# GEGLU on one core with split products: half of a set of operand sums made on VectorE, unit 4's S3 T3 divided, and pass two's second products next to each other

## The chip, the core and the metric

The kernel runs on one core of a Trainium2 chip. The core has a matrix engine (TensorE, PE in the profile; its weight loads are listed apart as PEld), a vector engine (VectorE, DVE), a scalar engine (ScalarE, ACT) and a general engine (GpSimd, POOL). SyncE (SP) issues the DMAs here. The engines each run their own instructions in the order in which they were written and wait for each other by semaphores. The metric is the time of one execution on the device in microseconds, as a median over runs.

## The reference

```python
def reference(x, w_gate, w_up, w_down):
    g = jnp.einsum("bsd,df->bsf", x, w_gate)
    u = jnp.einsum("bsd,df->bsf", x, w_up)
    h = _gelu(g) * u
    return jnp.einsum("bsf,fd->bsd", h, w_down)
```

x is 2048 x 1024, w_gate and w_up are 1024 x 3584, w_down is 3584 x 1024, all bfloat16; `_gelu` is the tanh form.

## The kernel before

**Split products.** The matrix products are made by a Strassen-Winograd scheme: a product of two 2 x 2 block matrices takes seven block products in place of eight, on sums of blocks. The sums of weights are called S1 to S4, the sums of x T1 to T4 (`sums_s`, `sums_t`); `tb` is a copy of a block of x. Raw blocks are 16-bit, sums are f32 (in the matmul format fp32r). Some of the seven products are themselves divided once more in the same manner, into seven halves of two matmuls each (`inner`, `half`) in place of one product of four matmuls for each of the four outputs (`product`, `whole`).

**Passes and units.** x is two passes p of 1024 rows. The columns of w_gate and w_up are 14 units u of 256 columns. Units 0 to 2 are worked off singly, for one pass at a time (`items`, `unit`, `whole_p4`). From `JOINT = 3` on, both passes of a unit are worked off jointly: units 3 to 13, with the products S4 Tb (steps X1 to X7) and A22 T4 (K1 to K7) divided. From unit `DIVIDED7 = 5` on, S3 T3 (H1 to H7) is divided too; before that it is H2, H3 and H4, made of whole products (16 matmuls for both passes and both weights). Behind the units follows the product with w_down (`down`).

**Order.** The order inside a joint unit is a text, `SEQUENCE` (`SEQUENCE_FIRST` for unit 3), of which each word issues some instructions. Upper-case words are matmuls: `P1pi` and `S`, `G` are products of raw 16-bit blocks (P1: four words of four matmuls; `S0 S1` are the second raw products of pass one, `G0 G1` those of pass two), `P6pi`, `P5pi`, X, H and K are f32. Lower-case words are single steps of DVE and ACT: `y5`, `kz1`, `kz6`, `v11` and so on copy a bank (ACT); `e00`, `e10`, `e01` copy what has been added up so far in the bank z into the bank of another output (ACT); `ga`, `gb`, `ha`, `hb` are gelus (ACT); `x..`, `c11a`, `e11`, `e10y` add (DVE); `m..` multiply and issue the store (DVE, SP). A word with `-` belongs to the unit before. `@` words are side work (`side_work`): sums of weights on POOL, loads, stores.

z and y are two of the eight banks of accumulation memory: X1, X6, X7 and H1, H6, H7 add up in z, X5 and H5 stand in y; in the K products the two are exchanged. H7 adds into z behind `e10`, which reads it.

**Sums of sums.** To divide a product, the sums T must be split into further sums: for tb and t4 three sums n1, n2, n4 (`split_b`) and one more, written over b12 (`split_b_rest`), for each of two k; all on POOL, 128 x 512 each. For t3 this is `split_b3`, in three parts (0 and 1: three sums each, 2: the two rests): part 0 at `@t4.1` of the unit before `DIVIDED7`, parts 1 and 2 at `@s3` of that unit. The weights' side is `half_sums`, two sums of 128 x 256 in each of two parts, at `@tb`, `@t3`, `@t4`. The sums n have places of their own (`place_n`, `more_room`) or slots of a common ring of 58 (`slot`).

The split of tb's rest and of t4 stands in the last single item, (0, 1): in `p4`, around `whole_p4`, that is ten POOL instructions ahead of unit 3:

```python
            def p4(c12):
                times(p, 2 * u, 1, gelu(c12[0]), c12[1])
                if n == len(items) - 1:
                    split_b_rest("tb")
                    more_room()
                    split_b("t4")
                whole_p4(u, p, banks[0], ss[u], ahead_of_p4, behind_p4)
                if n == len(items) - 1:
                    split_b_rest("t4")
```

Lines of the profile: L127 is the one line that issues every matmul, L106 every DVE tensor operation, L109 every one of POOL, L123 a copy out of a bank on ACT, L364 a copy into a bank, L373 and L221 gelus.

Of the kernel before, what the change touches and what calls it, by code (L numbers as in the profile page):

```python
# [10 lines left out]
def kernel(  # L11
# [19 lines left out]
    ADD, SUB, MUL = ALU.add, ALU.subtract, ALU.mult  # L31
# [14 lines left out]
    NWARM = 7  # L46
    JOINT = 3
    AHEAD = {(0, -2): 2, (0, -1): 2, (0, 1): 1, (1, -2): 1}
    DIVIDED7 = 5
    STAY = range(11, 14)  # L50
    KEEPS = [(u, n) for u in range(5, NU) for n in range({7: 2, 9: 2, 11: 2, 13: 3}.get(u, 1))]
    H, Q, R2 = NJ // 2, N // 2, range(2)
# [55 lines left out]
    def pool(out, a, b, op):  # L108
        nc.gpsimd.tensor_tensor(out=out, in0=a, in1=b, op=op)  # L109
# [190 lines left out]
    def blocks(name, k):  # L300
        return [T[p][name][h + k] for h in (0, 2) for p in range(2)]

    def split_b(name):
        n = ns[name] = [[], [], [], []]
        for k in range(2):
            b11, b12, b21, b22 = blocks(name, k)
            n1, n2, n4 = [place_n() for _ in range(3)]
            pool(n1, b12, b11, SUB)
            pool(n2, b22, n1, SUB)
            pool(n4, b21, n2, SUB)  # L310
            for got, t in zip(n, (n1, n2, b12, n4)):
                got.append(t)

    def split_b_rest(name):
        for k in range(2):
            b11, b12, b21, b22 = blocks(name, k)
            pool(b12, b22, b12, SUB)

    def split_b3(part):
        n = ns.setdefault("t3", [[], [], [], []])  # L320
# [13 lines left out]
    def half(ps, lhs, rhs, fresh=False):  # L334
# [2 lines left out]

    SEQUENCE = (
# [7 lines left out]
    ).split()  # L346

    SEQUENCE_FIRST = (
# [4 lines left out]
    ).split()  # L353

    def joint_ops(u, E, F):
# [85 lines left out]

        if u < DIVIDED7:
            for name in ("H1", "H5", "H6", "H7", "e00", "e10", "e01", "y5", "e11", "e10y"):
# [482 lines left out]
    sums, ns = {}, {}  # L926
    items = [(1, 0), (2, 0), (2, 1), (1, 1), (0, 1)]
# [41 lines left out]
    def load_next(u):  # L969
        if u < NU:  # L970
            ws[u] = load_w(u, u % 2 == 1)
# [13 lines left out]
    def side_work(u, what):  # L985
        def made(kind, n):
            if (u, n) in keeps:
                kind(keeps[u, n])

        more = u + 1 < NU  # L990
        name, part = what[:2], int(what[3:]) if what[2:3] == "." else None
        if what == "start":
            if u == JOINT:
                load_next(u + 1)
            made(fetch_wd, 1)
        elif what == "keep":
            made(keep_whole, 0)
        elif what == "store":
            if more:
                made(store_made, 0)  # L1000
            made(fetch_wd, 2)
        elif what == "s3":
            if u == DIVIDED7:
                split_b3(1)
                split_b3(2)
            if u > JOINT:
                new_s(u, "s3")
        elif name == "tb":
            if u > JOINT:
                half_sums(u, name, part)  # L1010
        elif name == "t3":
            if u >= DIVIDED7:
                half_sums(u, name, part)
            if more and part == 1:
                made(keep_whole, 1)
            if not more and part == 0:
                made(store_made, 0)
        elif what == "t4.0" and not more:
            half_sums(u, name, 0)
            half_sums(u, name, 1)  # L1020
        elif what == "t4.1" and not more:
            for n in range(1, 3):
                made(keep_whole, n)
        elif name == "t4":
            half_sums(u, name, part)
            if u == JOINT and part == 0:
                fetch_next(u)
            if u == DIVIDED7 - 1 and part == 1:
                split_b3(0)
        elif name in ("s1", "s2", "s4"):  # L1030
            if more:
                new_s(u + 1, what)
        elif what == "late":
            made(store_made, 1)
            if u > JOINT:
                fetch_next(u)
        elif what == "end":
            load_next(u + 2)
        if not more:
            last_loads(what)  # L1040
# [27 lines left out]
    with tc.manual_schedule(engines={ENG.Activation}):  # L1068
        for n, (u, p) in enumerate(items):
            first = n == 0  # L1070
            def after_p5():
                at_p5(n)

            def aside(part):
                if first and part < 0:
                    rest_of_0(part + 2)
                if first and part == 0:
                    t.make("t4")
                for v in loads.get((n, part), ()):
                    ws[v] = load_w(v, True)  # L1080
                turn_some(AHEAD.get((n, part), 0))
                if (n, part) == (1, -2):
                    two_sums("t2", XL[:, KH:], "t1")
                    two_sums("t3", XL[:, KH:], XL[:, :KH])

            def mid():
                if "sa" not in ss[u]:
                    ss[u]["sa"] = sums_s(loaded(u), pool)["how"]["sa"](None)

            def ahead_of_p4():  # L1090
                if n == 0:
                    raw_of(2, 0, even, cc)()
                elif n == 1:
                    p1 = [raw_first(e, 1, loaded(v)) for e, v in ((Eb, 2), (D, 1))]
                    raw_second(K, 1, loaded(2))
                    finish_raw(2, 1, K, p1[0])

                    T[1]["tb"] = spots["tb"]
                    for k in range(KH):
                        nc.scalar.copy(out=spots["tb"][k], in_=XT[1, 1][KH + k])  # L1100
                    new_room(0, 1, *["t4"] * KH, *["n"] * 3)
                    two_sums("t4", xT[1][:, KH:], "t2")
                    new_s(0, "s1", "s2", "s3", "s4")

                    def second_half():
                        raw_second(K, 1, loaded(1))
                        finish_raw(1, 1, K, p1[1])

                    nxt["c11"] = second_half
                elif n == 3:  # L1110
                    raw_of(0, 1, Ea, D)()

            def behind_p4():
                if "c11" in nxt:
                    nxt.pop("c11")()

            def p4(c12):
                times(p, 2 * u, 1, gelu(c12[0]), c12[1])
                if n == len(items) - 1:
                    split_b_rest("tb")  # L1120
                    more_room()
                    split_b("t4")
                whole_p4(u, p, banks[0], ss[u], ahead_of_p4, behind_p4)
                if n == len(items) - 1:
                    split_b_rest("t4")

            if first:
                banks = odd, cc, dd
                late = lambda: add(cc, nxt["p1"])
            else:  # L1130
                banks = (Eb, D, K) if n == 3 else (Ea, K, D)
                late = None
            unit(u, p, banks, ss[u], late, after_p5, aside, mid, p4)
            ss[u].pop("sa")
            if n == 1:
                Ea, Eb, K, D = Eb, D, K, Ea
            elif n == 3:
                Ea, Eb, K, D = Ea, K, D, Eb

        E, F = [Eb, K], [D, Ea]  # L1140
        last = None
        for u in range(JOINT, NU):
            now = joint_ops(u, E, F)
            steps = SEQUENCE_FIRST if u == JOINT else SEQUENCE
            for name in steps:
                if name[0] == "@":
                    side_work(u, name[1:])
                elif name[0] != "-":
                    now[name]()
                elif last:  # L1150
                    last[name]()
            last = now
            E, F = F, E
        for name in SEQUENCE:
            if name[0] == "-":
                last[name]()
# [51 lines left out]
```

## Time and profile before

| what | value |
|---|---|
| median of three runs | 526.39 us (526.26 to 526.95) |
| the profiled execution | 526.39 us, span 524.6 us |
| granted clock of TensorE | 1.00 throughout |
| unit 3, 4, 5, 6 (between the first weight loads of each, 83.49 to 179.88) | 24.26, 24.34, 23.90, 23.89 us |
| POOL busy in units 5 and 6 | 23.43 and 23.27 us |
| ten POOL sums ahead of unit 3 | from 85.40 to 98.39 us |

The span is the time from the first to the last instruction of the program; 1.8 us of the measured time lie around it. The profile gives for each engine the share of busy time, the chain of instructions that ended last (each followed back to what released it), the waits, and the instructions in order of time. In groups of instructions the tile names follow the program: `bank` is a bank, `w` and `xT` are raw weights and raw x, `s` sums of weights, `h`, `t`, `n` places of sums of x.

### The profile page before, as it was taken

How to read it: one execution, taken by the hardware profiler on the slowest of the kernel's cores; microseconds unless marked ns; L12 is line 12 of the kernel's file. 1: busy time of each engine (PE TensorE's matmuls, PEld its weight loads, DVE VectorE, ACT ScalarE, POOL GpSimd, SP SyncE). 2: the span in 40 equal slices, each digit the busy share in tenths (PEclk: the TensorE clock that was granted, in tenths of full speed). 3: DMA queues.
4: the chain of work that ended last, by engine and by line, in shares of the span. 5: the costliest groups of instructions: out<-in, count | busy, mean ns of one | idle time of the engine just before them, and what ended most of it. 6: DMA issues, size and time to landing. Idle time of an engine off the chain costs nothing.

```text
span 524.6 us, 7866 instructions
## 1 busy us (share of the span) xinstructions
PE 518.7 (99%) x2356; PEld 368.0 (70%) x2389; DVE 390.6 (74%) x598; ACT 293.6 (56%) x542; POOL 336.9 (64%) x339
## 2 busy tenths in 40 slices
PE   9999999999999999999999999999999999999997
PEld 5576877767667676767677676754788885488887
DVE  2984553687888989897988889897789226967934
ACT  3556655676778687878787787851135602142430
POOL 1079999998999999999999999840000000000594
PEclk9999999999999999999999999999999999999999
DMA  9961323032625457373727444999976999993732
GB/s 252 213 166 52 89 84 111 32 109 92 191 81 181 123 180 230 112 239 111 233 92 231 163 159 159 343 374 415 385 259 212 394 398 353 392 327 101 238 133 71
DMA packets 102730, 105.91 MB, mean 202 GB/s; under 512 B 19360, under 2 KB 80800, under 8 KB 102688
## 3 DMA queue, kind: packets, MB, share of 16 engines
q1 hardware_dynamic: 102688, 105.41, 61.4%
q8 instruction: 19, 0.31, 0.3%
q14 instruction: 23, 0.19, 0.1%
HBM read 72.61 MB, written 29.62 MB: 195 GB/s over the span
## 4 chain that ended last, share of the span: by engine, by line
PE 98%; DMA 1%; issue 0%; SPq 0%; DVE 0%
PE bank L127 98%; DMA xn<-in_x_dram 1%; SPq L797 0%; PE bank L804 0%; DVE st L106 0%
## 5 line engine op out<-in xcount | busy, mean ns | idle before, releaser
L127 PE MATMUL bank<-h,s 128*128 128x512 f32 x500 | 132.6, 395 | 0.0
L109 POOL TENSOR_TENSOR q<-q 128x256 fp32r<-128x256 f32 x28 | 26.6, 984 | 144.4 <-DMA q<-td 143.8
L127 PEld LDWEIGHTS bank<-h,s 128*128 128x128 f32 x500 | 93.9, 188 | 21.1
L127 PE MATMUL bank<-xT,w 128*128 128x512 bf16 (+1 forms) x446 | 106.8, 376 | 1.5
L127 PEld LDWEIGHTS <-w 128*128 128x128 bf16 x504 | 45.4, 98 | 59.1 <-issue 11.9
L109 POOL TENSOR_TENSOR s<-w 128x512 fp32r<-128x512 bf16 (+1 forms) x76 | 77.8, 1040 | 10.4 <-DMA w<-in_w_gate_dram 10.3
L127 PE MATMUL bank<-t,s 128*128 128x512 f32 x276 | 76.5, 400 | 0.0
L127 PE MATMUL bank<-q 128*128 128x512 f32 x264 | 65.6, 390 | 0.0
L127 PEld LDWEIGHTS bank<-t,s 128*128 128x128 f32 x276 | 51.9, 188 | 12.1
L127 PEld LDWEIGHTS bank<-q 128*128 128x128 f32 x264 | 49.6, 188 | 10.4
L123 ACT COPY p<-bank 128x512 f32<-128x512 f32 x72 | 40.6, 589 | 28.9 <-PE bank L127 28.6
L106 DVE TENSOR_TENSOR q<-h,h 128x512 fp32r<-128x512 bf16 x56 | 38.3, 684 | 16.8 <-DMA h<-hd 16.8
L123 ACT COPY u<-bank 128x512 f32<-128x512 f32 x62 | 35.8, 589 | 21.1 <-PE bank L127 21.0
L109 POOL TENSOR_TENSOR s<-s,s 128x256 fp32r<-128x256 f32 x60 | 44.8, 769 | 1.6
L106 DVE TENSOR_TENSOR xz<-bank,xz 128x512 f32<-128x512 f32 x44 | 30.2, 691 | 18.2 <-PE bank L127 14.6
L127 PEld LDWEIGHTS <-h 128*128 128x128 bf16 x224 | 21.7, 98 | 26.5 <-issue 0.5
L109 POOL TENSOR_TENSOR s<-w,s 128x512 fp32r<-128x512 bf16 (+1 forms) x37 | 39.4, 1081 | 0.0
L109 POOL TENSOR_TENSOR s<-s,w 128x512 fp32r<-128x512 f32 (+1 forms) x37 | 37.3, 1024 | 0.9
L118 ACT CAST tb<-raw 128x512 fp32r<-128x512 bf16 x28 | 16.9, 632 | 36.0 <-DMA raw<-in_w_down_dram 26.5
L109 POOL TENSOR_TENSOR m<-raw,m 128x512 fp32r<-128x512 bf16 x28 | 34.5, 1234 | 2.2
L106 DVE TENSOR_TENSOR bank<-bank,u 128x512 f32<-128x512 f32 x49 | 33.7, 688 | 0.0
L106 DVE TENSOR_TENSOR v<-bank,v 128x512 f32<-128x512 f32 x44 | 29.2, 684 | 2.1 <-PE bank L127 1.7
(122 smaller groups left out, 911.7 us busy)
## 6 DMA issues: line engine op xcount, KB each, us to landing
raw<-in_w_down_dram SPq DMA_DIRECT2D x68, 256.0 KB, 4.0
q<-td SPq DMA_DIRECT2D x66, 256.0 KB, 5.4
td<-m SPq DMA_DIRECT2D x42, 256.0 KB, 2.8
hd<-o SPq DMA_DIRECT2D x80, 128.0 KB, 1.7
h<-hd SPq DMA_DIRECT2D x17, 512.0 KB, 6.9
hd<-h SPq DMA_DIRECT2D x30, 128.0 KB, 1.7
h<-hd SPq DMA_DIRECT2D x5, 768.0 KB, 9.0
out_dram<-st SPq DMA_DIRECT2D x30, 128.0 KB, 4.6
```

What stands on the lines that cost most here:

```text
L106: nc.vector.tensor_tensor(out=out, in0=a, in1=b, op=op)
L109: nc.gpsimd.tensor_tensor(out=out, in0=a, in1=b, op=op)
L118: nc.scalar.copy(out=t, in_=src)
L123: nc.scalar.copy(out=t, in_=ps)
L127: nc.tensor.matmul(ps, lhsT=lhs, rhs=rhs, start=start, stop=stop, skip_group_check=True)
```

## The change

`DIVIDED7` goes from 5 to 4: unit 4 makes H1 to H7 too, with its side work (the four half sums at `@t3`) and with `split_b3` one unit earlier, so that part 0 falls into unit 3 and parts 1 and 2 into unit 4.

`split_b` and `split_b_rest` take an engine and a choice of k. The ten sums of tb and t4 leave `p4` and stand at `@start` of unit 3: tb's rest (two) and t4's three sums for k = 0 on DVE, t4's three for k = 1 and t4's rest (two) on POOL.

`SEQUENCE` has another order in the middle. Before, with the side work left out: `H5 P511 c11b gb y5 m11a H6 H2 v11 m12a K1 e10 x11 G0 kz1 m12b H7 f1 H3 v00+ K6 e01 e11 G1 hb`. After: `H5 H6 y5 c11b gb e10 P511 m11a H2 K1 v11 m12a x11 f1 H7 kz1 m12b H3 v00+ G0 G1 K6 e01 e11 hb`. So G0 and G1 follow each other directly, H6 comes ahead of P511, `e10` ahead of P511 as well, and H7 comes directly behind K1. `SEQUENCE_FIRST` is only broken into lines in another way.

```diff
-    DIVIDED7 = 5
+    DIVIDED7 = 4
...
-    def split_b(name):
-        n = ns[name] = [[], [], [], []]
-        for k in range(2):
+    def split_b(name, eng=pool, some=range(2)):
+        n = ns.setdefault(name, [[], [], [], []])
+        for k in some:
             b11, b12, b21, b22 = blocks(name, k)
             n1, n2, n4 = [place_n() for _ in range(3)]
-            pool(n1, b12, b11, SUB)
-            pool(n2, b22, n1, SUB)
-            pool(n4, b21, n2, SUB)
+            eng(n1, b12, b11, SUB)
+            eng(n2, b22, n1, SUB)
+            eng(n4, b21, n2, SUB)
...
-    def split_b_rest(name):
-        for k in range(2):
+    def split_b_rest(name, eng=pool, some=range(2)):
+        for k in some:
             b11, b12, b21, b22 = blocks(name, k)
-            pool(b12, b22, b12, SUB)
+            eng(b12, b22, b12, SUB)
...
-        "x6y X4 xz7 P611 x00 v10 x01 sg H1 X3 @room ga @t3.1 x7y S1 u211 x10 "
-        "e00 H5 @t4.0 P511 @free c11b gb y5 m11a H6 @t4.1 H2 v11 m12a K1 e10 x11 G0 @s1 kz1 m12b "
-        "H7 f1 H3 v00+ K6 e01 @late e11 G1 hb @s2 e10y kz6 H4 v10+ K5 sh K2 ha2 v01+ K7 ky5 m11b "
...
+        "x6y X4 xz7 P611 x00 v10 x01 sg H1 X3 @room ga @t3.1 x7y S1 u211 x10 e00 H5 @t4.0 H6 y5 @free "
+        "c11b gb e10 P511 m11a H2 @t4.1 K1 v11 m12a x11 f1 @s1 H7 kz1 m12b H3 v00+ G0 G1 K6 e01 @late "
+        "e11 hb @s2 e10y kz6 H4 v10+ K5 sh K2 ha2 v01+ K7 ky5 m11b K3 @s4 K4 kz7 @end "
...
             if u == JOINT:
                 load_next(u + 1)
+                split_b_rest("tb", dve)
+                split_b("t4", dve, range(1))
+                split_b("t4", pool, range(1, 2))
+                split_b_rest("t4")
...
                 if n == len(items) - 1:
-                    split_b_rest("tb")
                     more_room()
-                    split_b("t4")
                 whole_p4(u, p, banks[0], ss[u], ahead_of_p4, behind_p4)
-                if n == len(items) - 1:
-                    split_b_rest("t4")
```

On the engines this comes to two matmuls fewer, seven DVE instructions and four ACT copies more, one POOL instruction fewer (five less, four more), and the same transfers in the same order on SP.

10 rows, old and new, of tables (SEQUENCE, SEQUENCE_FIRST) are left out of this document.

## The prediction

> **What bounds the kernel now.** I read the page first: its share of busy time, the chain that ended last, then who waited for whom, and last the stretches of single units.
>
> ```profile
> span 524.6 us, 7866 instructions
> PE 518.7 (99%) x2356; PEld 368.0 (70%) x2389; DVE 390.6 (74%) x598; ACT 293.6 (56%) x542; POOL 336.9 (64%) x339
> PE 98%; DMA 1%; issue 0%; SPq 0%; DVE 0%
> ```
>
> The reader is to see that TensorE (PE) is busy 99% of the span and that the chain is PE for 98%. It runs matmul after matmul, and nothing else sets the end. The waits of the weight loads confirm it:
>
> ```profile
> PEld L127 <- issue: 12.4, 47, 0.3
> DVE p L106 <- PE bank L127: 9.6, 1, 9.6
> ```
>
> The only repeated pause of the weight loads is 0.26 us ahead of a group of 16-bit loads, 47 times, and it is put down to no other engine. VectorE (DVE), by contrast, once sits idle for 9.6 us; that is at the end of the last single item, just ahead of unit 3. So a gain must come from fewer or closer matmuls, and a loss from an engine that newly comes too late for PE.
>
> The stretches of units 4, 5 and 6 (cut at the first weight load of each; unit 4 begins at 107.75):
>
> ```profile
> 107.75:132.09 24.34, 24.24 (x107) 17.09 (x108) 21.12 (x32) 16.99 (x32) 22.41 (x24) 1.00 0.28 87
> 132.09:155.99 23.90, 23.80 (x105) 16.72 (x107) 20.21 (x32) 18.42 (x35) 23.43 (x25) 1.00 0.44 137
> 155.99:179.88 23.89, 23.78 (x105) 16.72 (x106) 21.12 (x34) 18.55 (x35) 23.27 (x25) 1.00 0.45 144
> ```
>
> Columns are time, then busy time and count of PE, PEld, DVE, ACT, POOL, and the granted clock, which is 1.00. Unit 4, the last undivided one, lasts 24.34 us; the divided ones 23.89. GpSimd (POOL) works 23.3 of 23.9 us, so it is the engine to watch.
>
> The weight loads of unit 5 and of unit 3 in order of time (start, length, what, count):
>
> ```profile
> 92.88 1.41 PEld L127 LDWEIGHTS <-w 128*128 128x128 bf16 x8 [0.26 <-issue]
> ...
> 99.18 1.41 PEld L127 LDWEIGHTS <-w 128*128 128x128 bf16 x8 [0.26 <-issue]
> ```
>
> ```profile
> 146.45 0.55 PEld L127 LDWEIGHTS <-w 128*128 128x128 bf16 x4 [0.26 <-issue]
> ...
> 150.08 0.55 PEld L127 LDWEIGHTS <-w 128*128 128x128 bf16 x4 [0.26 <-issue]
> 150.74 1.11 PEld L127 LDWEIGHTS bank<-h,s 128*128 128x128 f32 x5
> 151.89 0.19 PEld L127 LDWEIGHTS bank<-w,s 128*128 128x128 f32 x1
> 152.35 0.55 PEld L127 LDWEIGHTS <-w 128*128 128x128 bf16 x4 [0.27 <-issue]
> ...
> 155.99 0.98 PEld L127 LDWEIGHTS <-w 128*128 128x128 bf16 x6 [0.26 <-issue]
> ```
>
> At 146.45, 150.08 and 152.35 stand three groups of four 16-bit matmuls: S1, G0 and G1. Between G0 and G1 there are only six f32 matmuls. In unit 3, which has the other sequence, S0 S1 and G0 G1 stand together as two groups of eight.
>
> **What a switch of type costs.** In long undisturbed runs the loads start 0.2267 us apart in f32 and 0.216 in 16 bit. From 150.08 to 152.35 lie 4 + 6 matmuls: 4 x 0.216 + 6 x 0.2267 = 2.224, and the trace has 2.274, 0.050 more. From 152.35 to 155.99 lie 4 + 12: 3.584 against 3.633, 0.049 more. So a group of four costs about 0.05 us: part at its head, part in the nine or so f32 loads behind it, which start 0.228 to 0.238 apart. Unit 3's groups of eight: 92.88 to 99.18 (8 + 20) 6.262 against 6.300, and 99.18 to 107.75 (8 + 30) 8.529 against 8.567: 0.038 each. Per unit: 106 matmuls make 32 x 0.216 + 74 x 0.2267 = 23.69, and 23.89 is measured: 0.20 for four groups.
>
> **The change, part by part.**
>
> Unit 4 divided: four whole products of four matmuls (16) become seven halves of two (14). Two f32 matmuls are gone: 24.34 - 23.89 = 0.45 us saved, which agrees with 2 x 0.2267. This is on PE's path.
>
> G0 next to G1 (units 4 to 13, ten units): one group fewer in each. Bounds: nothing, if an eight costs as much as two fours; and 0.050 + 0.049 - 0.038 = 0.061 by unit 3's eights, the nearest row. I take 0.05, a whole group's cost, because the f32 work behind the eights of unit 3 is another than in later units: 10 x 0.05 = 0.50 us.
>
> Five sums from POOL to DVE at unit 3's start: two of Tb's rest and three of T4. On POOL such a sum takes 1.27 to 1.30 us, so POOL has 6.4 us less. On DVE a sum of this shape takes 0.68 with POOL idle (q<-h,h). None of the type with both operands f32 in SBUF stands there but o<-v,v, which takes 0.68 to 1.59 beside POOL. Five thus take 3.4 to 7.9 us and begin when DVE is done with the last h, at 84.4; the next DVE step, c11a, starts at 94.02. They end by 92.3. The cover is the 9.6 us of waiting for PE; without it they would hold back c11a and, behind it, the seed of f0 that G0 needs. The first user of Tb's rest is X7, behind S0 S1 (92.88), and of T4's sums the K products (from 101.6).
>
> A rule that speaks against this, from the Trainium skill, page "SBUF — State Buffer", section "Who interferes with whom": a VectorE instruction with two SBUF inputs and a GpSimd instruction that reads SBUF exclude each other, and the later one waits for the whole of the other. The spread of o<-v,v (0.68 to 1.59) agrees. Strictly alternating, five pairs would take 5 x (1.29 + 0.69) = 9.9 us and end at 94.3, 0.3 us past c11a's start; the seed of f0 comes at 97.62 after a stretch in which DVE idles 1.3 us, so the sum stays the same by the rule.
>
> S3 T3 in unit 4: DVE gets two more steps (0.69 each), ACT four copies (0.59), in the unit where both have most room (DVE 21.1 of 24.3, ACT 17.0): nothing. POOL gets four half sums (0.75 + 2.1 = about 3.0), and the splitting of T3 comes one unit earlier: three sums (4.0) at unit 3's end instead of unit 4's, five (6.9) at unit 4's start instead of unit 5's. POOL against before: -6.4 at unit 3's start, -2.4 at its end, +4.5 ahead of unit 4's S3, +7.5 behind its four half sums, +3.5 at its end, -3.4 in unit 5. Who needs it: S3, now done at 111.09 to 113.4, moves to 115.6 to 117.9, and the first half sum to 118.7. In unit 5, H1 begins 13.2 us and H5 15.0 us behind the unit's start; in unit 4 that is 121.0 and 122.8. Some 4.1 us are left, against 1.7 where unit 5 does this now (145.45 to 147.11). Hidden; if the 6.4 were not given back, PE would stand 2.3 us once.
>
> New order of H6, y5, e10, P511, H2, K1, H7: this costs PE nothing itself, but H7 adds into the bank that e10 reads, so PE waits for e10 there. At present e10 ends at 173.89 (its row 173.29, 0.60) and the next load that needs it starts at 174.64: 0.75 to spare. In the new order y5 starts 0.65 behind H5's last load (as kz1 does behind K1: load 149.63, copy 150.28), and the gelu gb stands between y5 and e10. Chain: 0.65 + 0.48 (copy to gelu, 175.52 to 176.00) + 0.53 (gelu to copy, 100.11 to 100.64) + 0.60 = 2.26 behind H5's last load. On PE eleven loads lie between that and H7: 11 x 0.2267 = 2.49. It leaves 0.23; the trace has a load starting 0.13 behind ACT's end (122.18 to 122.31) with no pause. Zero, with 0.1 us to spare. Queued behind H7 are all later matmuls. K6 now stands behind G1, so that seven loads (1.59) instead of eleven lie between its last load and K7, which adds into the bank that kz6 copies: 0.65 + 0.59 = 1.24, so 0.35 are left of 1.2 (kz6's end at 153.19, K7's load at 154.39): zero too. P511 comes two loads and G0 four f32 loads later; behind G0 waits the gelu hb, whose product on DVE (178.66) starts 2 us after hb ends (176.60): hidden.
>
> DMA: SP issues the same transfers in the same order, with seven more waits for slots. The weights for unit 5 are issued at 104.49 and used from 132.09, so a few us there are hidden.
>
> Sum: 0.45 + 0.50 = 0.95 us less. The profiled execution took 526.39 with a span of 524.6 (1.8 around it), and 526.39 is also the median of the runs. So 525.44, or -0.18%.
>
> **Rivals.**
> 1. Groups gain by unit 3's row or somewhat more: 0.45 + 10 x 0.061 = 1.06, 525.33. For it: the eights are the same instructions. Against: what follows them differs. Some spread of a median (runs lie 526.26 to 526.95) adds to this case.
> 2. Only the two matmuls count, since the cost goes with the number of 16-bit loads: 525.94. Against it: 20 loads would then cost 0.25, and four groups with 32 loads cost 0.20 in all.
> 3. H7 waits for e10 (the slower side). If ACT is held up by one more of its instructions between H5 and e10 (0.48), PE stands 0.48 - 0.23 + 0.06 = 0.3 us in each of ten units: 525.44 + 3.1 = 528.5. It decides from 0.1 us of stall a unit, which eats the gain; from 0.2 the kernel is slower by more than can be measured. For: the spare time falls from 0.75 to some 0.1 to 0.2, and K7's from 1.2 to 0.35. Against: ACT is idle ahead of y5 and its durations hardly vary.
> 4. POOL too late in unit 4, since it is locked out by DVE: at most the 2.3 us above, 527.7. Against: 4.1 us to spare.
>
> **How the numbers follow.** About 0.2% (1.05 us) is what a measurement of this kernel can tell from no change. Forecast (525.35 to 525.8) 0.48; rival 1, 0.35; rival 2, 0.06; rival 3, 0.08; rival 4, 0.03. Faster by over 0.2%: rival 1 and a little of the forecast's lower edge, 0.37. Slower: rivals 3 and 4 where they pass the bound, 0.09. The rest, 0.54, is within. The range runs from 525.15 (rival 1 with 0.2 of spread) to 526.0 (rival 2).
>
> **What would show it.** After: some 37 pauses of the weight loads put down to issue in place of 47; unit 4 at 23.84 like all later ones, which fall from 23.89 by 0.04 to 0.06; the DVE's wait of 9.6 us cut to 2 to 6; no wait of PE for ACT ahead of H7, nor for POOL at H1 and H5 of unit 4. I am wrong if units of 24 us and more appear with a pause ahead of H7, or if the later units keep 23.89.

## The result and the profile after

| | before | after |
|---|---|---|
| median, 20 runs each | 526.70 us (526.26 to 527.45) | 525.84 us (525.16 to 526.47) |
| ratio | | 0.998, 95% interval 0.9974 to 0.9987 |
| span of the profiled execution | 524.6 us | 524.1 us |
| first weight load of unit 3 to the first behind unit 13 | 263.64 us | 262.59 us |
| unit 4 | 24.346 us | 23.833 us |
| each of units 5 to 12 | 23.893 us | 23.833 us |

The changed kernel is faster by 0.2%; the interval is 0.7 to 1.4 us of 526.7, and the medians lie 0.86 us apart. 525.44 was forecast, 0.95 us less than the 526.39 that before had then. One execution of a kernel further below, e2_old_order, took 1128.56 us and stands in no ratio. The units' lengths, here and below, are taken between the first weight loads of two units, in the one execution of each kernel that was profiled. Apart from single units that are named, they repeat to 0.001 us from unit to unit (units 9 and 12 of e4 differ by 0.007), and tell far more than the spread of the runs does.

The page after, the same three lines as before:

```profile
span 524.1 us, 7920 instructions
PE 519.8 (99%) x2387; PEld 368.7 (70%) x2387; DVE 396.7 (76%) x605; ACT 292.4 (56%) x546; POOL 335.4 (64%) x338
PE 98%; DMA 1%; SPq 0%; DVE 0%; issue 0%
```

PE still makes up 98% of the chain: nothing else sets the end. The weight loads show the two matmuls that are gone (2389 and 2387). The count of matmuls itself rises, from 2356 to 2387: some of their records are missing in the first trace. The span shrank by only 0.5 us, because these two executions differ at the start: the chain of waits in order of time has the first load of x in it, once 4.03 and once 4.60 us long (start, length, what; before first, after second).

```profile
2.12 4.03 DMA xn<-in_x_dram
```

```profile
2.13 4.60 DMA xn<-in_x_dram
```

So every clock reading after unit 0 is 0.57 us later in the second trace, at a step that the change does not touch: the same start of unit 3 lies between 83.38 and 84.34 in the ten traces. Lengths of stretches can be compared, starts cannot. From unit 3 to the end of unit 13, PE needs 1.053 us less.

The waits of the weight loads after:

```profile
PEld L127 <- issue: 8.9, 34, 0.3
PEld L127 <- DMA td<-m: 0.8, 3, 0.3
PEld L127 <- DMA w<-in_w_up_dram: 0.3, 1, 0.3
PEld L127 <- DMA out_dram<-st: 0.3, 1, 0.3
PEld L127 <- DMA hd<-h: 0.3, 1, 0.3
```

The pause ahead of 16-bit loads stands here too under the names of transfers that happened to land then; all lines together are 40 pauses, against 50 before (47 put down to issue and three to transfers). Ten are gone, one for each unit from 4 to 13. No line has POOL, DVE or ACT in it.

The stretches of units 4, 5 and 6 after (time; then busy time and count of PE, PEld, DVE, ACT, POOL; clock):

```profile
108.31:132.15 23.84, 23.84 (x108) 16.80 (x107) 21.34 (x33) 18.59 (x36) 23.37 (x25) 1.00 0.26 82
132.15:155.98 23.83, 23.83 (x107) 16.79 (x107) 20.68 (x33) 18.12 (x35) 23.12 (x26) 1.00 0.46 144
155.98:179.81 23.83, 23.83 (x107) 16.79 (x106) 20.86 (x33) 18.21 (x35) 22.63 (x25) 1.00 0.44 143
```

Unit 4 has become as long as the others, and all have become shorter. The weight loads of unit 5 show where (start, length, what, count):

```profile
146.50 0.55 PEld L127 LDWEIGHTS <-w 128*128 128x128 bf16 x4 [0.26 <-issue]
...
149.91 0.87 PEld L127 LDWEIGHTS bank<-h,s 128*128 128x128 f32 x4
151.04 1.41 PEld L127 LDWEIGHTS <-w 128*128 128x128 bf16 x8 [0.26 <-issue]
152.57 0.19 PEld L127 LDWEIGHTS bank<-h,s 128*128 128x128 f32 x1
...
155.98 0.55 PEld L127 LDWEIGHTS <-w 128*128 128x128 bf16 x4 [0.26 <-issue]
```

S1 is a group of four as before; G0 and G1 are one group of eight with one pause. From 151.04 to 155.98 lie 8 + 14 loads, 4.940 us by the single starts. At 0.216 and 0.2267 they would take 4.902: the eight costs 0.038, as much as those of unit 3.

The five sums on VectorE and, beside them, POOL's own, at the start of unit 3:

```profile
84.92 2.05 DVE L106 TENSOR_TENSOR h<-h 128x512 fp32r<-128x512 f32 x2
86.89 1.76 DVE L106 TENSOR_TENSOR h<-h,t 128x512 fp32r<-128x512 f32 x1
88.69 1.67 DVE L106 TENSOR_TENSOR h<-h 128x512 fp32r<-128x512 f32 x1
90.39 1.67 DVE L106 TENSOR_TENSOR w<-t,h 128x512 fp32r<-128x512 f32 x1
94.58 0.69 DVE L106 TENSOR_TENSOR p<-bank,p 128x512 f32<-128x512 f32 x1 [2.52 <-PE bank L127]
```

```profile
86.38 1.73 POOL L109 TENSOR_TENSOR w<-h,t 128x512 fp32r<-128x512 f32 x1
88.18 1.62 POOL L109 TENSOR_TENSOR w<-h,w 128x512 fp32r<-128x512 f32 x1
89.89 1.63 POOL L109 TENSOR_TENSOR w<-t,w 128x512 fp32r<-128x512 f32 x1
91.48 2.97 POOL L109 TENSOR_TENSOR h<-h 128x512 fp32r<-128x512 f32 x2
```

Five sums take VectorE 7.1 us (84.92 to 92.06), and c11a still waits 2.5 us for PE behind them. Each of POOL's takes 1.5 to 1.7 us now; alone it took 1.27 to 1.30.

### The profile page after: what moved, and what is told of

Same layout as the page of the kernel before. It is cut to its first block, busy times and chain, and to the rows that moved or that the text cites. A ratio compares the mean times of both kernels' runs of the same rounds, so it can differ in the third digit from the quotient of the medians.

```text
span 524.1 us, 7920 instructions
## 1 busy us (share of the span) xinstructions
PE 519.8 (99%) x2387; PEld 368.7 (70%) x2387; DVE 396.7 (76%) x605; ACT 292.4 (56%) x546; POOL 335.4 (64%) x338
## 4 chain that ended last, share of the span: by engine, by line
PE 98%; DMA 1%; SPq 0%; DVE 0%; issue 0%
PE bank L127 98%; DMA xn<-in_x_dram 1%; SPq L796 0%; PE bank L803 0%; DVE st L106 0%
## 5 line engine op out<-in xcount | busy, mean ns | idle before, releaser
L127 PE MATMUL bank<-t,s 128*128 128x512 f32 x272 | 75.4, 399 | 0.0
L127 PEld LDWEIGHTS bank<-q 128*128 128x128 f32 x264 | 49.6, 188 | 10.4
L109 POOL TENSOR_TENSOR s<-s,s 128x256 fp32r<-128x256 f32 x63 | 49.1, 802 | 1.6
```

The lines of the kernel that those rows point to most:

```text
L127: nc.tensor.matmul(ps, lhsT=lhs, rhs=rhs, start=start, stop=stop, skip_group_check=True)
```

## The experiments

All lengths are in us; the ratio is to the kernel before, with its 95% interval.

| run | what differs | unit 4 | units 5 to 12 | ratio |
|---|---|---|---|---|
| before | | 24.346 | 23.893 | |
| after | the whole change | 23.833 | 23.833 | 0.998 (0.9974 to 0.9987) |
| e1_ten_on_pool | no sum on VectorE | 26.586 | 23.833 | 1.0036 (1.0022 to 1.005) |
| e2_old_order | sequence of before | 23.893 | 23.893 | 0.9991 (0.9981 to 1.0) |
| e3_order_alone | new sequence alone | 24.286 | 23.833 (unit 6: 23.886) | 0.9992 (0.9982 to 1.0001) |
| e4_e10_behind_v11 | e10 later on ACT | 24.453 | 24.453 to 24.460 | 1.0095 (1.0075 to 1.0115) |
| e5_h3_between | H3 between G0 and G1 | 23.887 | 23.887 | 0.999 (0.9979 to 1.0001) |
| e6_sums_alone | the five sums alone | 24.346 | 23.893 | 0.9994 (0.9983 to 1.0005) |
| e7_ten_on_dve | all ten on VectorE | 23.833 | 23.833 (unit 5: 23.820) | 1.0022 (1.001 to 1.0035) |
| e8_rest_on_dve | two on VectorE | 25.087 | 23.833 | 1.0004 (0.9993 to 1.0016) |

**The parts one by one.** First the change without the new order:

```diff
-        "c11b gb e10 P511 m11a H2 @t4.1 K1 v11 m12a x11 f1 @s1 H7 kz1 m12b H3 v00+ G0 G1 K6 e01 @late "
...
+        "e00 H5 @t4.0 P511 @free c11b gb y5 m11a H6 @t4.1 H2 v11 m12a K1 e10 x11 G0 @s1 kz1 m12b "
+        "H7 f1 H3 v00+ K6 e01 @late e11 G1 hb @s2 e10y kz6 H4 v10+ K5 sh K2 ha2 v01+ K7 ky5 m11b "
```

> The changed kernel with the sequence of before: unit 4 divided, the sums on VectorE, but G0 and G1 apart again. Theory (each part acts by its matmul stream alone, and they add up): unit 4 falls from 24.346 to 23.893 us like units 5 to 12, which stay at 23.893; 0.45 us faster than before. Rival (unit 4 gains by the order too, or the order is needed for the division): units differ from 23.89 or show a pause at H1, H5 or H7 of unit 4.

Unit 4 is 23.893 and so are the others, except unit 10 with 23.880. Dividing unit 4 takes 0.453 us out of it and nothing anywhere else. Then the new order without the rest:

> The kernel before with the new sequence alone: unit 4 undivided, ten sums on POOL. Theory (a group of eight costs 0.039 us where two of four cost 0.050 and 0.049): units 5 to 12 at 23.833, unit 4 at 24.286, ten units with 0.060 less: 0.60 us faster than before. Rival (a whole group's cost, 0.05, as predicted): 23.843, 0.50 us. Rival (the order gains by waits that it removes, which need the division of unit 4 or POOL's lead): units stay at 23.89.

Unit 4 is 24.286, the others are 23.833: 0.060 less in each, as the price of unit 3's groups of eight had it, not 0.050. One unit is an exception, unit 6 with 23.886; it is taken up in the last section. 0.453 and 10 x 0.060 make 1.053, which is what the whole change shows. At last the move of the five sums without the rest:

> The kernel before with five of the ten sums on VectorE alone: unit 4 undivided, the old sequence. Theory (the move is hidden on both sides and gains nothing by itself): unit 4 24.346, units 5 to 12 23.893 us, the same time as before within 0.1 us of PE's stream; POOL ends its five some 4.5 us earlier. Rival (POOL's lead shortens waits that the profile does not name): units under 23.89.

Unit 3 to unit 13 takes 263.64 us, the same as before: the move alone gains nothing and costs nothing.

**What the move is for.** All ten sums on POOL again, in a kernel that is otherwise the changed one:

```diff
-                split_b_rest("tb", dve)
-                split_b("t4", dve, range(1))
+                split_b_rest("tb", pool)
+                split_b("t4", pool, range(1))
```

> The changed kernel with all ten sums of Tb and T4 on POOL at the start of unit 3, as many on POOL as before the change. Theory (the five sums on VectorE are what makes unit 4's division free): POOL ends these sums some 4.5 us later (98.4 before the change, 94.4 after it, on a start 0.6 us later), so unit 4's first S3 sum comes at about 123.8 in place of 119.31, and H1 (121.54) waits 2.3 us, H5 and H6 a little more: 2.5 to 2.9 us in unit 4 alone, once. Unit 4 about 26.5 us, the others 23.83, the whole 1.5 to 1.9 us slower than the kernel before. Rival (POOL's lead is not needed, the move gains nothing): unit 4 stays at 23.83 and the kernel is 1.05 us faster than before, like the changed one.

Unit 4 is 26.586, 2.75 longer, and the weight loads say why:

```profile
123.24 0.30 PEld L127 LDWEIGHTS bank<-t,s 128*128 128x128 f32 x2 [2.35 <-POOL s L109]
...
125.17 0.30 PEld L127 LDWEIGHTS bank<-n,s 128*128 128x128 f32 x2 [0.35 <-POOL s L109]
...
125.99 0.30 PEld L127 LDWEIGHTS bank<-n,s 128*128 128x128 f32 x2 [0.52 <-POOL s L109]
```

These are H1, H5 and H6 of unit 4, each waiting for a sum of weights from POOL. (The waits hold the usual gaps between loads, and the pair of loads behind each starts closer, 0.30 in place of 0.41, so that they come to 2.75.) The division would have cost 2.75 us and brought 0.45. With two sums on VectorE:

```diff
-                split_b("t4", dve, range(1))
+                split_b("t4", pool, range(1))
```

> The changed kernel with only Tb's two rests on VectorE, eight sums on POOL. Theory (POOL's lead is what counts, about 0.9 us for each sum moved: with none moved PE waited 2.35 us at H1 of unit 4, with five moved 2.1 us were left there): with two moved, H1 waits some 0.5 us, H5 and H6 a little; unit 4 at 24.0 to 24.9 us, once, the others 23.833. Rival (any part of the move is enough): unit 4 at 23.833.

Unit 4 is 25.087, 1.25 us of waiting: half of the 2.75 or so is left, more than the 0.2 to 1.1 expected. POOL ended its sums at 97.20 with unit 3 begun at 83.90, that is 13.3 behind the start, against 14.9 with ten on POOL (98.28 less 83.38) and 10.4 in the changed kernel (94.45 less 84.06). The two sums gave it 1.6 us and took 1.5 us off the wait; five give 4.5 us, enough for the 2.75. So the lead of POOL is what counts, and it comes at less than 1.3 us a sum. Then all ten on VectorE:

```diff
-                split_b("t4", pool, range(1, 2))
-                split_b_rest("t4")
+                split_b("t4", dve, range(1, 2))
+                split_b_rest("t4", dve)
```

> The changed kernel with all ten sums on VectorE. In the changed kernel five took 7.1 us (84.92 to 92.06), 1.2 to 1.8 each, beside POOL's. Theory (a sum with two SBUF operands waits for POOL's instruction, so it costs as much on VectorE as on POOL): ten take 13 to 17 us and end at 98 to 102, c11a (94.6 now) is held back by 3 to 7 us, the seed of f0 comes after it, and PE waits ahead of G0 of unit 3 by up to 3 us, once: 0 to 3 us slower than the changed kernel. Rival (0.69 us each, as where POOL is idle): they end at 91 to 92 and nothing waits.

```profile
91.31 1.67 DVE L106 TENSOR_TENSOR w<-h,w 128x512 fp32r<-128x512 f32 x1
93.01 1.65 DVE L106 TENSOR_TENSOR w<-t,w 128x512 fp32r<-128x512 f32 x1
94.59 3.34 DVE L106 TENSOR_TENSOR h<-h 128x512 fp32r<-128x512 f32 x2
97.85 0.68 DVE L106 TENSOR_TENSOR p<-bank,p 128x512 f32<-128x512 f32 x1
```

This is VectorE at the start of unit 3 of that kernel. The ten end at 97.93, 13.1 us behind their begin at 84.87, and c11a, the last line, begins 3.3 us later than in the changed kernel. Unit 3 takes 26.33 us in place of 24.25: 2.07 us of it are lost, and the kernel is slower than before. PE stands at X7, not at G0:

```profile
98.56 0.63 ACT L372 ACTIVATE p<-p 128x512 f32<-128x512 f32 x1 [4.30 <-DVE p L106]
...
100.04 0.60 ACT L123 COPY xz<-bank 128x512 f32<-128x512 f32 x1
```

```profile
100.71 0.76 PEld L127 LDWEIGHTS bank<-h,s 128*128 128x128 f32 x4 [2.19 <-POOL s L109]
```

The first line is the gelu `ha`, which waits for c11a; the copy `xz6` of the bank z stands behind it on ACT and ends at 100.64, and X7 adds into z. The profile names POOL, but POOL's last sum ahead of this ended at about 100.07, and ACT's copy is what ends just before the load. The cover of 9.6 us is real, and it ends between five and ten sums.

**What a group costs.** H3 put between G0 and G1:

```diff
-        "c11b gb e10 P511 m11a H2 @t4.1 K1 v11 m12a x11 f1 @s1 H7 kz1 m12b H3 v00+ G0 G1 K6 e01 @late "
+        "c11b gb e10 P511 m11a H2 @t4.1 K1 v11 m12a x11 f1 @s1 H7 kz1 m12b G0 H3 v00+ G1 K6 e01 @late "
```

> The changed kernel with H3 (two f32 matmuls) put between G0 and G1, so that there are two groups of four again, two loads apart, at otherwise the same place. Theory (a group's cost belongs to the group, 0.050 for a four and 0.039 for an eight, however few f32 loads follow it): units 4 to 12 go from 23.833 back to 23.893 us, 0.6 us in all. Rival (the cost lies in the nine or so slower f32 loads behind a group, so that two loads between the groups cut most of it off): units at 23.85 to 23.87. Rival (the new order gained by the places of H7 and H3, not by the group): units stay at 23.833.

The units are 23.887: 0.054 of the 0.060 is lost again. The weight loads of unit 5 have G0 and G1 as two groups with a pause each:

```profile
150.47 0.55 PEld L127 LDWEIGHTS <-w 128*128 128x128 bf16 x4 [0.26 <-issue]
151.13 0.41 PEld L127 LDWEIGHTS bank<-h,s 128*128 128x128 f32 x2
151.82 0.55 PEld L127 LDWEIGHTS <-w 128*128 128x128 bf16 x4 [0.28 <-issue]
```

By the single starts, the stretch from G0 to G1 (4 + 2 loads) is 1.351 us, 0.034 more than at the two rates, and the one from G1 to the next unit (4 + 14) 4.096, 0.058 more. The first group cannot spend all of its slower f32 loads on two loads, and what is left over appears behind the next group: the slower f32 loads run on for ten there, where behind a group of four in the kernel before it is seven. The cost belongs to the group, nearly whatever follows.

**The narrowest place in the new order.** In the changed kernel ACT does y5, gb and e10 one behind the other (unit 6; the lines of the gelu and of the copy into a bank are L372 and L363 here, one less than in the kernel before):

```profile
171.87 0.59 ACT L123 COPY y<-bank 128x512 f32<-128x512 f32 x1 [0.92 <-PE bank L127]
172.36 0.64 ACT L372 ACTIVATE xz<-xz 128x512 f32<-128x512 f32 x1
172.89 0.59 ACT L363 COPY bank<-bank 128x512 f32<-128x512 f32 x1
```

e10 ends at 173.48, and H7's first load starts at 173.74, 0.26 later, with no pause; it is the same in every unit but 4, where it is 0.21. To see whether this wait is real, e10 was moved behind v11:

```diff
-        "c11b gb e10 P511 m11a H2 @t4.1 K1 v11 m12a x11 f1 @s1 H7 kz1 m12b H3 v00+ G0 G1 K6 e01 @late "
+        "c11b gb P511 m11a H2 @t4.1 K1 v11 e10 m12a x11 f1 @s1 H7 kz1 m12b H3 v00+ G0 G1 K6 e01 @late "
```

> The changed kernel with e10 moved behind K1 and v11 in the sequence, so that ACT does the copy v11 ahead of it. Theory (H7 waits for e10; the spare time is 0.26 us): v11 starts 0.65 us behind P511's last load, e10 0.49 later and takes 0.59, so it ends 1.73 us behind that load, while H7's turn is five loads (1.13 us) behind it: 0.6 to 0.7 us of pause ahead of H7 in each of the ten units, units of 24.4 to 24.55, 6 to 7 us slower than the changed kernel. Rival (PE does not wait there, because some later step carries the wait): units stay at 23.83.

Every unit from 4 on is 24.453 or 24.460, 0.62 longer. ACT and the matmuls of unit 6 in this kernel:

```profile
173.94 0.59 ACT L123 COPY v<-bank 128x512 f32<-128x512 f32 x1 [0.26 <-PE bank L127]
174.42 0.59 ACT L363 COPY bank<-bank 128x512 f32<-128x512 f32 x1
```

```profile
174.19 0.61 PE L127 MATMUL bank<-t,sg 128*128 128x512 f32 x2
175.16 1.17 PE L127 MATMUL bank<-h,s 128*128 128x512 f32 x4 [0.35 <-ACT bank L363]
```

K1 is the first matmul line, H7 the second, and H7 waits for the copy of L363, which is e10. e10 ends at 175.01 and H7's weights start to load at 175.12, so the signal takes 0.11 us, and of the 0.26 in the changed kernel 0.15 was truly to spare (0.10 in unit 4).

None of the kernels that ran is faster than the changed one, and the runs do not point to one that would be: what is left of the cost of groups (three in a unit) seems tied to steps of VectorE and ACT between S1, G0 and G1. That was not tried.

## Why the prediction was right, step by step

**What bounds the kernel** held: in units 3 to 13 PE has no other wait after the change than the switch of type, and the parts add up to 0.001 us (0.453 + 10 x 0.060 = 1.053) where no unit has an odd pause.

**Unit 4 divided**, 0.45 forecast: 0.453 (e2).

**G0 next to G1** is the term that was sized wrongly. I took "0.05, a whole group's cost, because the f32 work behind the eights of unit 3 is another than in later units". It is 0.060 in each of ten units (e3): an eight costs 0.038 in later units as well, and the bound that I named from unit 3's own rows was the value. The step from 0.95 to 1.053 is all of this but 0.003. It is rival 1's sum (1.06), so the change lies between my forecast and that rival; a ratio of 0.998 cannot tell the two apart, the units' lengths can. The time itself, 525.84, lies nearest to rival 2 (525.94), but only because before took 526.70 beside it, 0.31 more than the 526.39 that the forecast started from. Rival 2 (only the two matmuls) is out by e3: there the later units fall by 0.060 with the new order alone.

**The five sums** were rightly called hidden on VectorE, for 3.4 to 7.9 us forecast and 7.1 measured, and c11a's wait fell from 9.6 to 2.5. If they had come too late, they would have cost at X7, by way of `ha` and `xz6` on ACT (e7), and not through the seed of f0 and G0 as I had it. What I got wrong is POOL's side. I took 6.4 us off POOL and let the lock act on VectorE alone; but POOL's own five were stretched from 1.29 to 1.5 to 1.7 each, the three small sums ahead of them from 2.10 (e1) to 2.54, and the lead was 4.5 us. So 2.1 us were left at H5 of unit 4 (half sum done at 121.26, load at 123.33) where 4.1 was forecast. Less still was left at H6, which the new order puts directly behind H5 and which I did not reckon:

```profile
120.51 0.75 POOL L109 TENSOR_TENSOR s<-s 128x256 fp32r<-128x256 f32 x1
121.33 2.14 POOL L109 TENSOR_TENSOR s<-s,s 128x256 fp32r<-128x256 f32 x3
```

```profile
123.33 0.87 PEld L127 LDWEIGHTS bank<-n,s 128*128 128x128 f32 x4
```

Its half sum, the first of the three, is done at 122.08 and its first load, the third of the four, starts at 123.78: 1.7 us. e1 and e8 agree with that, not with 2.1: their POOL ends the sums 4.5 and 2.9 us later behind the unit's start, and unit 4 is 2.75 and 1.25 longer. It cost nothing because the margin was wide, not because it was reckoned rightly, and e1 shows that rival 4's price was near: 2.3 forecast without the move, 2.75 measured. The Trainium skill's page "SBUF — State Buffer", section "Who interferes with whom", says that it is the order of issue that decides which of the two engines blocks. The trace agrees in that both rows are longer than alone (0.68 and 1.29), and the prediction should have charged both. The strict turns that the prediction worked out by that section's rule do not come out: VectorE's last three sums start 1.70 to 1.80 apart (86.89, 88.69, 90.39), not the 1.98 of both lengths together, and the five took 7.1 us, not 9.9.

**e10 and H7**: 0.23 forecast, 0.26 measured (0.21 in unit 4), 0.15 with the signal's 0.11 taken off. Rival 3 needed one more ACT instruction there, at 0.3 us a unit. e4, with another shift, has 0.62 a unit, so the mechanism exists and the spare time was what kept it out. K7 behind kz6: 0.35 forecast, 0.32 to 0.37 measured.

**Pauses**: some 37 put down to issue were forecast and 34 are there; counted with those under the names of transfers, 50 became 40, ten fewer as forecast.

## What to carry to other kernels

Where the matrix engine is the bound, count its instructions and the places where their type changes, and price both from the distances of the weight loads; rows of the same kernel in another order (here unit 3) give the price better than a mean. Work moved to another engine can gain nothing by itself and still be what another part of the change stands on: look for who is late without it. And read the spare time of each new wait in both engines' rows before moving a word of the order.

## What had not been expected

H7 is not the only narrow place: X1, at the start of a unit, is about as narrow, and no list of waits above had it. In e3, unit 6 is 0.053 longer than its neighbours. At its start, VectorE spends 1.70 us on one product of two SBUF operands, which in the trace before takes 0.68 to 1.59:

```profile
156.10 1.70 DVE L106 TENSOR_TENSOR o<-v,v 128x512 bf16<-128x512 f32 x1
```

X1 of the same unit then has the only odd pause; VectorE's second `kz` sum, which X1 needs, starts at 161.12, takes 0.68 and so ends 0.12 ahead of X1's load:

```profile
161.92 0.30 PEld L127 LDWEIGHTS bank<-tb,s 128*128 128x128 f32 x2 [0.21 <-issue]
```

In the trace before, the same sum ends 0.20 to 1.20 us ahead of X1's load, in the changed kernel 0.22 (unit 8) to 1.14. The profile does not name VectorE for this pause, but the ten traces together do: of their 100 units from 4 to 13, four have X1's load late, and in these four it starts 0.114 to 0.116 behind the sum's end (e1 unit 4, e2 unit 10, e3 unit 6, e7 unit 5), in the other 96 at least 0.126. In the same four, and in no other, the product `o<-v,v` ahead ends later than 0.95 us behind the unit's start; it took 1.64 to 1.72 there. So X1 waits for VectorE, and the long product fits as the reason; it was not tried by itself. Such a pause need not make the unit longer, since the pair of loads behind it starts closer (0.30 in place of 0.41): the units in e2 and e7 are even 0.013 shorter, the one in e3 is 0.053 longer.
